# Moving an FFN down product from TensorE to VectorE, with a new start and a re-cut weight stream, in a fused attention and FFN kernel

## Chip, cores and metric

The kernel runs on one core of one Trainium2 chip. The metric is the device time of one execution in microseconds (us). The kernel before takes 263.93 us, the median of 3 runs (263.43 to 264.33).

The engines are named as in the profile: PE is TensorE (PEld its weight loads), DVE is VectorE, ACT is ScalarE, POOL is GpSimd, SP is SyncE, which issues most of the transfers. In the listings "L75" is the line of one helper through which nearly every instruction is issued, so groups are told apart by their tiles (`output<-inputs`) and not by line.

## The reference, cut to what matters

Sequence 2048, width 1024, FFN width 3584, bf16. The output mixes a linear attention block and an FFN that is applied to one single row of x, the one with the largest router logit:

```python
g = sigmoid((x * gate_w).sum(-1))             # one gate per row
pq, pk = phi(x @ Wq), phi(x @ Wk)             # phi(t) = (t > 0 ? t + 1 : exp(t)) + 1e-6
a = (pq @ (pk.T @ v)) / (pq @ pk.sum(0)) @ wo # per head, 32 heads of 32
r = x @ w_r;  i = argmax(r)
h = silu(x[i] @ w_gate) * (x[i] @ w_up)       # 3584 values of one row
b = x;  b[i] += sigmoid(r[i]) * (h @ w_down)
out = g * a + (1 - g) * b
```

Nearly all of the arithmetic is attention. The FFN has almost none, but it moves 22 MB of weights.

## The kernel before: the parts that matter here

PE takes its work in program order: the start (two x tiles transposed, first K products), K and V for x tiles 0 to 3, router product, then for each of the x tiles 4 to 15 a K pair, a V pair, the accumulation of K'V (`kvacc`, 8 small matmuls) and some Q units. FFN weight tiles are slipped in between. A "unit" is eight 128x512 matmuls into one of four PSUM work buffers.

```python
Q_PER_T = {4: 2, 5: 1, 6: 1, 7: 2, 8: 1, ...}
FFN_PER_T = {6: 8, 8: 8, 10: 8, 12: 8, 13: 1, 14: 7, 15: 7}  # weight tiles after x tile t
FFN_DEPTH = 10                                # weight tiles in flight

# the start (abridged): K weights of 512 columns in four pieces, then the rest
load_x(0, 1); load_w0(0); load_x(1, 1)
for c2 in range(1, 4): load_w0(c2)
load_x(2, 2)
for nb in range(1, 4): load_wkv(nb)

# FFN gate and up: the row stands in column 0 of a padded 128x32 weight;
# four column groups of the array each take 512 of the 2048 columns of a tile
for j in range(nr):                           # nr = 4, in the second half 3
    pe.matmul(ps[32*j : 32*j+32, :], lhsT=xs_pad[:, c, :],
              rhs=wt[:, 512*j : 512*j+512], ..., tile_position=(0, 32*j))

# FFN down: 28 row blocks x 4 column groups = 112 matmuls of 256 columns
pe.matmul(ps[32*j : 32*j+32, :], lhsT=hT_pad[:, k, :],
          rhs=wt[:, 1024*kk + 256*j : 1024*kk + 256*j + 256], start=(k == 0), stop=(k == 27), ...)

# gate logits to token columns: four fp32 products with a selection matrix
pe.matmul(gl_ps[:, 4*b : 4*b+4], lhsT=rg_f[:, b*P : (b+1)*P], rhs=selg[:], ...)

# copy of x (4 MB) into the tensor in which the FFN row is replaced later
ffn_prefetch()                                # ten weight tiles
cp = nc.sync.dma_start(out=xp[:], in_=x2d)    # ... then the copy, in the same queue
```

`phi` costs two ACT steps and one DVE step for each K and Q unit; that DVE step is what frees the PSUM buffer.

Of the kernel before, what the change touches and what calls it, by code (L numbers as in the profile page):

```python
# [21 lines left out]
P = 128  # L22
# [8 lines left out]
N_WARM = 7  # L31
Q_PER_T = {4: 2, 5: 1, 6: 1, 7: 2, 8: 1, 9: 1, 10: 2, 11: 1, 12: 1, 13: 2, 14: 1, 15: 0}
FFN_PER_T = {6: 8, 7: 0, 8: 8, 9: 0, 10: 8, 11: 0, 12: 8, 13: 1, 14: 7, 15: 7}
FFN_DEPTH = 10
# [4 lines left out]
def kernel(  # L39
# [66 lines left out]
    ps_acc = ph1.enter_context(tc.tile_pool(name="ps_acc", bufs=1, space=PSUM))  # L106
# [15 lines left out]
    def load_w0(c2):  # L122
        sp.dma_start(out=wkv[:, 2 * c2 : 2 * c2 + 2, 0:512], in_=wqkv_v[:, 2 * c2 : 2 * c2 + 2, D : D + 512])

    def load_wkv(nb):
        sp.dma_start(out=wkv[:, :, 512 * nb : 512 * nb + 512], in_=wqkv_v[:, :, D + 512 * nb : D + 512 * nb + 512])

    load_x(0, 1)
    load_w0(0)
    load_x(1, 1)  # L130
    for c2 in range(1, 4):
        load_w0(c2)
    load_x(2, 2)
    for nb in range(1, 4):
        load_wkv(nb)
# [27 lines left out]
    selg = const.tile([P, 4], F32)  # L163
    nc.gpsimd.memset(selg[:], 0.0)
    for j in range(4):
        nc.gpsimd.memset(sel4[32 * j : 32 * j + 1, j : j + 1], 1.0)
    pidx_i = const.tile([P, 4], I32)
    nc.gpsimd.iota(pidx_i[:], pattern=[[-32, 4]], base=-1, channel_multiplier=1)
# [6 lines left out]
    hT_pad = rt.tile([P, 28, 32], BF)  # L175
    nc.gpsimd.memset(hT_pad[:], 0.0)
# [3 lines left out]
    kvacc = [ps_acc.tile([P, 512], F32, name=f"kvacc{i}") for i in range(3)]  # L180
# [17 lines left out]
    def unit_T(t):  # L198
        xt = xnat[t]
        pst = ps_work.tile([P, D], BF, tag="w")  # L200
        for c in range(KC):
            pe.transpose(pst[:, c * P : (c + 1) * P], xt[:, c * P : (c + 1) * P], ident[:])
        dst = xT[:, :, t * P : (t + 1) * P]
        src = pst[:].rearrange("p (c s) -> p c s", c=KC)
        if t < 3:
            dve.tensor_copy(dst, src)
        else:
            act.copy(dst, src)
# [48 lines left out]
    kv_open(1)  # L257
    unit_T(0)
    warm(3)
    ps0 = ps_work.tile([P, 512], F32, tag="w")  # L260
    kv_mm(ps0, 0, 0, 0, 2)
    unit_T(1)
    ps1 = ps_work.tile([P, 512], F32, tag="w")
    kv_mm(ps0, 0, 0, 2, 4)
    warm(1)
    kv_mm(ps0, 0, 0, 4, 8)
    e00 = phi_exp(ps0[:])
    kv_mm(ps1, 1, 0, 0, 4)
    unit_T(2)
    kv_mm(ps1, 1, 0, 4, 8)  # L270
    unit_T(3)
    e01 = phi_exp(ps1[:])
    phi_dve(ps0[:], e00, pk_t[0][:, 0:512])
    phi_dve(ps1[:], e01, pk_t[1][:, 0:512])
    for t in (2, 3):
        unit_KV(t, 0)
    pidx_f = const.tile([P, 4], F32)
    dve.tensor_copy(pidx_f[:], pidx_i[:])
    dve.tensor_scalar(selg[:], pidx_f[:], 0.0, None, op0=ALU.is_equal)
# [7 lines left out]
    for nb in range(1, 4):  # L287
        for t in range(4):
            unit_KV(t, nb)
# [11 lines left out]
    act.copy(rg_f[:], rps[:])  # L301
    r_f = rt.tile([P, 512], F32)
# [35 lines left out]
    def router_part2():  # L338
        xs_ps = ps_ffn.tile([P, KC + 1], F32, tag="f")
        for c in range(KC):  # L340
            pe.matmul(xs_ps[:, c : c + 1], lhsT=xsel_row[0:1, c * P : (c + 1) * P], rhs=one_bf[0:1, 0:1],
                             start=True, stop=True)
        pe.matmul(xs_ps[:, KC : KC + 1], lhsT=ones_row[0:1, :], rhs=rmax_bf[0:1, 0:1], start=True, stop=True)
        dve.tensor_copy(xs_pad[:, :, 0], xs_ps[:, 0:KC])
        act.activation(sig[:], xs_ps[:, KC : KC + 1], ACTF.Exp, scale=-1.0)
        dve.tensor_scalar_add(sig[:], sig[:], 1.0)
        dve.reciprocal(sig[:], sig[:])
        gl_ps = ps_ffn.tile([P, NT], F32, tag="f")
        for b in range(4):
            pe.matmul(gl_ps[:, 4 * b : 4 * b + 4], lhsT=rg_f[:, b * P : (b + 1) * P], rhs=selg[:], start=True, stop=True)  # L350
        act.activation(gate[:].rearrange("p (j b) -> p j b", b=4), gl_ps[:].rearrange("p (b j) -> p j b", j=4),
                             ACTF.Exp, scale=-1.0)
        dve.tensor_scalar_add(gate[:], gate[:], 1.0)
        dve.reciprocal(gate[:], gate[:])
        dve.tensor_scalar(omg[:], gate[:], -1.0, 1.0, op0=ALU.mult, op1=ALU.add)


# [5 lines left out]
    def ffn_pieces():  # L363
        for half in range(2):
            nr = 4 if half == 0 else 3
            c0 = 2048 * half
            for wi, wmat in enumerate((B_w_gate, B_w_up)):
                wv = wmat.rearrange("(c p) f -> p c f", p=P)
                for c in range(KC):
                    def load(half=half, nr=nr, c0=c0, wv=wv, c=c):  # L370
                        wt = ffw.tile([P, 2048], BF, tag="ffw")
                        ld = nc.sync.dma_start(out=wt[:, 0 : 512 * nr], in_=wv[:, c, c0 : c0 + 512 * nr])  # L372
                        if not ffn_state.get("first"):
                            ffn_state["first"] = True
                            tc.add_manual_dep(ld.ins, xsel_ld[0].ins.name, SYNC, reason="row fetch before the weight stream")
                        return wt

                    def compute(wt, half=half, nr=nr, wi=wi, c=c):
                        if c == 0:
                            ps = ps_ffn.tile([P, 512], F32, tag="f")  # L380
                            ffn_state["ps"] = ps
                            if nr < 4:
                                dve.memset(ps[96:128, :], 0.0)
                        ps = ffn_state["ps"]
                        for j in range(nr):
                            pe.matmul(ps[32 * j : 32 * j + 32, :], lhsT=xs_pad[:, c, :], rhs=wt[:, 512 * j : 512 * j + 512],
                                             start=(c == 0), stop=(c == KC - 1), tile_position=(0, 32 * j))
                        if c == KC - 1:
                            if wi == 0:
                                eg = tmp.tile([P, 512], F32, tag="ffn_e", bufs=1)  # L390
                                act.activation(eg[:], ps[:], ACTF.Exp, scale=-1.0)
                                dve.tensor_scalar_add(eg[:], eg[:], 1.0)
                                dve.reciprocal(eg[:], eg[:])
                                dve.tensor_tensor(sg_t[half][:], ps[:], eg[:], op=ALU.mult)
                            else:
                                dve.tensor_tensor(h_bf[half][:], ps[:], sg_t[half][:], op=ALU.mult)

                                def h_transpose(half=half, nr=nr):
                                    hps = ps_ffn.tile([P, 16], F32, tag="f")
                                    for b in range(4):  # L400
                                        pe.matmul(hps[:, 4 * b : 4 * b + 4], lhsT=h_bf[half][:, b * P : (b + 1) * P],
                                                         rhs=sel4[:], start=True, stop=True)
                                    dst = hT_pad[:, 16 * half : 16 * half + 4 * nr, 0].rearrange("p (j b) -> p j b", b=4)
                                    src = hps[:].rearrange("p (b j) -> p j b", j=4)[:, 0:nr, :]
# [3 lines left out]
                                ffn_state["barrier"] = True  # L408
# [3 lines left out]
        for k2 in range(14):  # L412
            def load(k2=k2):
                wt = ffw.tile([P, 2048], BF, tag="ffw")
                nc.sync.dma_start(out=wt[:].rearrange("p (k n) -> p k n", k=2), in_=wdv[:, 2 * k2 : 2 * k2 + 2, :])
                return wt

            def compute(wt, k2=k2):
                if k2 == 0:
                    ffn_state["ps"] = ps_ffn.tile([P, 256], F32, tag="f", name="yps")  # L420
                ps = ffn_state["ps"]
                for kk in range(2):
                    k = 2 * k2 + kk
                    for j in range(4):
                        pe.matmul(ps[32 * j : 32 * j + 32, :], lhsT=hT_pad[:, k, :],
                                         rhs=wt[:, 1024 * kk + 256 * j : 1024 * kk + 256 * j + 256],
                                         start=(k == 0), stop=(k == 27), tile_position=(0, 32 * j))
                if k2 == 13:
# [10 lines left out]
    def ffn_prefetch():  # L439
        while len(inflight) < FFN_DEPTH:  # L440
            nxt = next(pieces, None)
            if nxt is None:
                return
            inflight.append((nxt[0](), nxt[1]))

    def ffn_step(n):
        pend = ffn_state.pop("pending", None)
        if pend is not None:
            pend()
            if ffn_state.get("stage2_next"):  # L450
                return
        for _ in range(n):
            if not inflight:
# [4 lines left out]
            if ffn_state.pop("barrier", False):  # L458
                ffn_state["stage2_next"] = ffn_state.get("n_h", 0) == 1
                ffn_state["n_h"] = ffn_state.get("n_h", 0) + 1  # L460
                return
# [4 lines left out]
    for t in range(4, NT):  # L466
        for nb in range(4):
            unit_KV(t, nb)
            if nb == 1 and t > 4:
                unit_KVACC(t - 1)  # L470
        nq = Q_PER_T[t]
        for i in range(nq):
            unit_Q(*q_units.popleft())
            if t == 4 and i == 0:
                router_part1()
                ffn_prefetch()
                cp = nc.sync.dma_start(out=xp[:], in_=x2d)
                tc.add_manual_dep(cp.ins, xsel_ld[0].ins.name, SYNC, reason="row fetch before the copy")
        if t == 5:
            router_part2()  # L480
        if t >= 6:
            ffn_step(FFN_PER_T[t])
# [148 lines left out]
```

## Time and profile before

| before | |
|---|---|
| time, median of 3 | 263.93 us |
| span of the profiled execution | 263.1 us |
| PE busy | 257.7 us, 98% |
| DVE busy | 116.1 us, 44% |
| PE waits for FFN weights | 0.6 us |

The prediction below shows the lines that carry this. Groups of PE instructions of the kernel before by shape (count | busy us, mean ns of one | idle before them):

```profile
L75 PE MATMUL ps<-wt,xs_pad 128*32 128x512 bf16 x112 | 8.0, 381 | 0.6 <-DMA wt<-in_B_w_gate_dram 0.4 <-DMA wt<-in_B_w_up_dram 0.2
L75 PE MATMUL yps<-wt,hT_pad 128*32 128x256 bf16 x112 | 3.4, 273 | 0.0
```

The busy column is the union of overlapping matmuls, which is why 112 matmuls of 381 ns each make 8.0 us. A better measure of a part, on an engine that never stops, is the distance between the start of one row of its timeline and the start of the next.

For comparing whole runs I cut the span at two PE rows: the start ends where the router product (`rps`) starts, the middle ends where the first product of denominators (`dps`) starts.

### The profile page before, as it was taken

The numbers are of one execution on the slowest core, as the hardware profiler recorded it, in microseconds if no ns is written. First come the engines' busy times: TensorE is split into PE (matmuls) and PEld (weight loads), VectorE is DVE, ScalarE is ACT, GpSimd is POOL, SyncE is SP. The second block draws the span as 40 slices with busy tenths as digits, with TensorE's granted clock in tenths as the row PEclk, the third lists the DMA queues.
The fourth block names the chain that finished last, engine by engine and source line by source line (L and its number), as shares of the span: only waits on it lengthen the run. The fifth ranks groups of instructions, "written<-read, shape, count | busy, mean of one in ns | idle before, by whom it ended". The sixth has DMA issues, their size and how long they took to land.

```text
span 263.1 us, 4003 instructions
## 1 busy us (share of the span) xinstructions
PE 257.7 (98%) x1541; PEld 122.0 (46%) x1541; DVE 116.1 (44%) x216; ACT 127.5 (48%) x201; POOL 47.9 (18%) x101
## 2 busy tenths in 40 slices
PE   7999999999999999999999999999999999999995
PEld 3444445445444445444444445544444444444443
DVE  1354005233181322328222222276995579964443
ACT  1286324555445534554634545257799751333310
POOL 7000001010000000000000000011997019970000
PEclk9999999999999999999999999999999999999999
DMA  6999990009996997019219807176000274455222
GB/s 175 351 298 208 250 319 0 0 3 340 410 518 230 376 348 298 0 49 362 109 41 302 298 0 267 54 236 226 0 2 0 80 229 149 138 185 159 82 80 80
DMA packets 33058, 47.71 MB, mean 181 GB/s; under 512 B 14152, under 2 KB 18640, under 8 KB 32976
## 3 DMA queue, kind: packets, MB, share of 16 engines
q1 hardware_dynamic: 32752, 47.32, 54.3%
q8 instruction: 12, 0.20, 0.3%
q0 software_dynamic: 256, 0.14, 0.2%
q14 instruction: 6, 0.05, 0.1%
q10 hardware_dynamic: 32, 0.00, 0.0%
HBM read 39.85 MB, written 8.39 MB: 183 GB/s over the span
## 4 chain that ended last, share of the span: by engine, by line
PE 81%; DMA 14%; SPq 2%; issue 0%; DVE 0%
PE ps L75 76%; DMA wt<-in_B_w_up_dram 12%; PE kvacc L75 2%; DMA wkv<-in_A_wqkv_dram 2%; SPq L372 2%; PE yps L75 1%; SPq L75 1%; PE dps L75 1%; PE rps L75 1%; PE pst L75 0%; DVE ot L75 0%; PE pt L75 0%; PE hps L75 0%; PE wps L75 0%
## 5 line engine op out<-in xcount | busy, mean ns | idle before, releaser
L75 PE MATMUL ps<-wkv,xT 128*128 128x512 bf16 x512 | 116.1, 380 | 0.1
L75 PEld LDWEIGHTS <-xT 128*128 128x128 bf16 x512 | 48.8, 98 | 57.0 <-issue 2.3
L75 ACT ACTIVATE u<-ps 128x512 f32<-128x512 f32 x64 | 38.2, 597 | 53.2 <-PE ps L75 52.5
L75 PE MATMUL ps<-xT,wq 128*128 128x512 bf16 x256 | 58.9, 379 | 0.0
L75 PE MATMUL ps<-m_sb,pq_all 128*128 128x512 bf16 (+1 forms) x264 | 55.6, 373 | 0.0
L75 DVE SCALAR_TENSOR_TENSOR pq_all<-ps,e 128x512 bf16<-128x512 f32 x32 | 21.8, 685 | 50.5 <-ACT e L75 50.5
L75 ACT ACTIVATE e<-u 128x512 f32<-128x512 f32 x64 | 40.4, 631 | 1.7
L75 PEld LDWEIGHTS <-pq_all 128*128 128x128 bf16 x264 | 25.8, 98 | 29.8 <-issue 0.4
L75 PEld LDWEIGHTS <-wq 128*128 128x128 bf16 x256 | 24.8, 98 | 29.9 <-issue 0.6
L545 POOL TENSOR_TENSOR pq_all<-pq_all,rb 128x512 bf16<-128x512 bf16 x32 | 36.0, 1170 | 7.4 <-DVE rb L75 7.4
L75 DVE SCALAR_TENSOR_TENSOR pk<-ps,e 128x512 bf16<-128x512 f32 x32 | 21.9, 686 | 32.5 <-ACT e L75 32.5
L75 ACT CAST vt<-ps 128x512 bf16<-128x512 f32 x32 | 18.8, 587 | 32.9 <-PE ps L75 32.9
L75 DVE SCALAR_TENSOR_TENSOR ot<-ps,gate,xg 128x512 bf16<-128x512 f32 (+1 forms) x33 | 23.7, 723 | 16.8 <-PE ps L75 15.0
L75 ACT ACTIVATE xg<-xt,omg 128x1024 f32<-128x1024 bf16 x16 | 18.2, 1147 | 25.9 <-DVE ot L75 25.9
L75 DVE STREAM_SHUFFLE rb<-rdp 128x512 f32<-128x512 f32 x32 | 22.2, 732 | 0.0
L217 POOL MEMSET vt<- 128x8 bf16 x16 | 1.9, 136 | 106.9 <-PE kvacc L75 106.9
L75 PEld LDWEIGHTS <-pk 128*128 128x128 bf16 x128 | 8.5, 98 | 3.3 <-issue 0.4
L75 PE MATMUL kvacc<-vt,pk 128*128 128x129 bf16 x128 | 9.7, 221 | 0.0
L75 ACT CAST m_sb<-ps 128x512 bf16<-128x512 f32 x16 | 9.3, 583 | 0.0
L75 PE MATMUL ps<-wt,xs_pad 128*32 128x512 bf16 x112 | 8.0, 381 | 0.6 <-DMA wt<-in_B_w_gate_dram 0.4
L431 POOL DMA_DIRECT2D xp<-brow x1 | 0.6, 573 | 38.5 <-DVE brow L75 38.5
L75 DVE RECIPROCAL rd<-dn 128x512 f32<-128x512 f32 x2 | 6.7, 3353 | 1.7 <-ACT dn L75 1.7
(99 smaller groups left out, 79.7 us busy)
## 6 DMA issues: line engine op xcount, KB each, us to landing
wt<-in_B_w_down_dram SPq DMA_DIRECT2D x14, 512.0 KB, 7.4
wt<-in_B_w_gate_dram SPq DMA_DIRECT2D x8, 512.0 KB, 8.9
wt<-in_B_w_up_dram SPq DMA_DIRECT2D x8, 512.0 KB, 18.7
xt<-xp SPq DMA_DIRECT2D x16, 256.0 KB, 2.7
out_dram<-ot SPq DMA_DIRECT2D x15, 256.0 KB, 2.0
wkv<-in_A_wqkv_dram SPq DMA_DIRECT2D x3, 1024.0 KB, 11.0
wt<-in_B_w_gate_dram SPq DMA_DIRECT2D x8, 384.0 KB, 5.9
wt<-in_B_w_up_dram SPq DMA_DIRECT2D x8, 384.0 KB, 5.2
```

Of the source, the lines that this page charges most:

```text
L75: inst = fn(*a, **k)
L217: nc.gpsimd.memset(vt_t[t][:, :, 128:129], 1.0)
L372: ld = nc.sync.dma_start(out=wt[:, 0 : 512 * nr], in_=wv[:, c, c0 : c0 + 512 * nr])
L431: nc.gpsimd.dma_start(out=xp[bass.ds(nonlocal_idx[0], 1), :].rearrange("o (j n) -> (o j) n", j=4), in_=brow[0:128:32, :])
L545: nc.gpsimd.tensor_tensor(sl, sl, rb[:], op=ALU.mult)
```

## The change

It does five things: K weights come row by row and serve two x tiles at once from the start; the down product becomes 28 multiply-adds on DVE, with a short fp32 sum over partitions on PE at the end; gate and up use four equal column groups in both halves (512, then 384 columns), four tiles at a time instead of eight; the gate logits reach their token columns through a small DRAM tensor, not through PE; and the copy of x is issued after the last FFN weight. The schedule of the FFN tiles follows (`FFN_PER_T`), with nine weight tiles in flight instead of ten. The aim is to take work off PE, which is busy for 98% of the span.

```diff
-N_WARM = 7
+N_WARM = 5
-FFN_PER_T = {6: 8, 7: 0, 8: 8, 9: 0, 10: 8, 11: 0, 12: 8, 13: 1, 14: 7, 15: 7}
-FFN_DEPTH = 10
+FFN_PER_T = {6: (0, 4), 7: (4, 4), 8: (4, 4), 9: (4, 4), 10: (4, 2), 11: (2, 2), 12: (1, 2), 13: (1, 2), 14: (1, 2), 15: (1, 0)}
+FFN_DEPTH = 9
@@ the start @@
+    def load_k(c):
+        sp.dma_start(out=wkv[:, c, 0:D], in_=wqkv_v[:, c, D : 2 * D])
     load_x(0, 1)
-    load_w0(0)
+    load_k(0)
     load_x(1, 1)
... (six K rows, x tile 2, two K rows, x tile 3, V in two halves)
+    first = [[ps_work.tile([P, 512], F32, tag="w", ...) for nb in range(2)] for t in range(2)]
... (K row c: two matmuls for x tile 0, two for x tile 1; x tiles through a PSUM pool of their own)
@@ gate logits @@
-        for b in range(4):
-            pe.matmul(gl_ps[:, 4 * b : 4 * b + 4], lhsT=rg_f[:, b * P : (b + 1) * P], rhs=selg[:], start=True, stop=True)
+    nc.sync.dma_start(out=gl_d[:], in_=rg_f[1:128:32, :])
+            ld = nc.sync.dma_start(out=gl[:].rearrange("p (j b) -> p j b", b=4), in_=gl_d[:].rearrange("j (b p) -> p j b", p=P))
@@ gate and up @@
-            nr = 4 if half == 0 else 3
-            c0 = 2048 * half
+            w = 512 if half == 0 else 384
+            c0 = 512 * half
-                        ld = nc.sync.dma_start(out=wt[:, 0 : 512 * nr], in_=wv[:, c, c0 : c0 + 512 * nr])
+                        ld = nc.sync.dma_start(out=wt[:, 0 : 4 * w].rearrange("p (j f) -> p j f", j=4),
+                                          in_=wv[:, c, :].rearrange("p (j f) -> p j f", j=4)[:, :, c0 : c0 + w])
@@ down product @@
-                        pe.matmul(ps[32 * j : 32 * j + 32, :], lhsT=hT_pad[:, k, :],
-                                         rhs=wt[:, 1024 * kk + 256 * j : 1024 * kk + 256 * j + 256],
-                                         start=(k == 0), stop=(k == 27), tile_position=(0, 32 * j))
+                    if i2 == 0 and kk == 0:
+                        dve.tensor_scalar(yacc[:], w, h1, None, op0=ALU.mult)
+                    else:
+                        dve.scalar_tensor_tensor(yacc[:], w, h1, yacc[:], op0=ALU.mult, op1=ALU.add)
+                if i2 == 13:
+                    for j in range(4):
+                        pe.matmul(ps[32 * j : 32 * j + 32, :], lhsT=ones_f[:], rhs=yacc[:, 256 * j : 256 * j + 256],
+                                  start=True, stop=True, tile_position=(0, 32 * j))
@@ copy of x @@
             if nxt is None:
+                if not ffn_state.get("copied"):
+                    cp = nc.sync.dma_start(out=xp[:], in_=x2d)
...
-                cp = nc.sync.dma_start(out=xp[:], in_=x2d)
@@ loop over x tiles @@
+            if nb == 1:
+                ffn_step(FFN_PER_T.get(t, (0, 0))[0])
```

In the new `FFN_PER_T` the first number is the tiles taken after the K pair of an x tile, the second those after its Q units.

## The prediction

> **What bounds the kernel now.** I read the busy table first, then the chain of work that ended last, then the waits of the matrix engine (engine, tile, releaser; us in total, times, longest).
>
> ```profile
> PE 257.7 (98%) x1541; PEld 122.0 (46%) x1541; DVE 116.1 (44%) x216; ACT 127.5 (48%) x201; POOL 47.9 (18%) x101
> PE 81%; DMA 14%; SPq 2%; issue 0%; DVE 0%
> ...
> PE ps L75 <- DMA wt<-in_B_w_gate_dram: 0.4, 1, 0.4
> PE ps L75 <- DMA wt<-in_B_w_up_dram: 0.2, 1, 0.2
> ```
>
> PE is busy for 257.7 of 263.1 us and, once started, waits only for FFN weights, twice, 0.6 us in all. The 14% of DMA in the chain is mostly the FFN weight stream, followed back from one of these short waits; it is not 14% that could be won. So time comes only from work taken off PE, from those 0.6 us, and from the first 10 us, where warm-up matmuls count as busy. Any new wait of PE counts in full.
>
> Next the timeline of PE at the parts that the diff touches (start, length in us):
>
> ```profile
> 61.35 1.02 PE L75 MATMUL gl_ps<-selg,rg_f 128*128 128x4 f32 x8
> 62.23 2.97 PE L75 MATMUL ps<-wkv,xT 128*128 128x512 bf16 x13
> ...
> 115.64 1.91 PE L75 MATMUL ps<-wt,xs_pad 128*32 128x512 bf16 x24
> 117.48 3.63 PE L75 MATMUL ps<-wkv,xT 128*128 128x512 bf16 x16
> ...
> 157.78 1.71 PE L75 MATMUL yps<-wt,hT_pad 128*32 128x256 bf16 x56
> 159.42 3.63 PE L75 MATMUL ps<-wkv,xT 128*128 128x512 bf16 x16
> ...
> 166.90 1.71 PE L75 MATMUL yps<-wt,hT_pad 128*32 128x256 bf16 x56
> 168.55 1.68 PE L75 MATMUL ps<-xT,wq 128*128 128x512 bf16 x7
> ```
>
> A part's cost on PE is from its start to the start of the next row: gate logits 0.88 us, eight weight tiles of the second FFN half 1.84 us, the down product 1.64 + 1.65 us. A unit of K, V or Q (eight 128x512 matmuls) costs 1.73 us by the same reading (3.45 for 16).
>
> Then the supply and the vector engine: stretches with GB/s at their end, and two vector groups.
>
> ```profile
> 11.00:17.00 6.00, 6.00 (x41) 3.08 (x40) 2.67 (x4) 4.29 (x8) 0.00 (x0) 1.00 1.09 348
> 60.00:72.00 12.00, 12.00 (x92) 6.06 (x93) 3.19 (x9) 6.17 (x12) 0.13 (x1) 1.00 1.00 396
> ...
> L75 DVE SCALAR_TENSOR_TENSOR pk<-ps,e 128x512 bf16<-128x512 f32 x32 | 21.9, 686 | 32.5 <-ACT e L75 32.5
> L75 DVE TENSOR_TENSOR kvbd<-kvacc,mask_bd 128x384 bf16<-128x384 f32 x2 | 1.1, 547 | 0.0
> ```
>
> The first stretch is K and V weights in runs of 1 KB: 348 GB/s. The second is FFN weights in runs of 4 KB: 396. The engines are saturated in both. The vector rows give the slope of a two-tensor operation: (686 - 547)/128 = 1.09 ns per column.
>
> **What the Trainium skill says.** (1) "VectorE: DVE Perf Modes", sections on the errata and on the tier table: a two-tensor operation with an fp32 operand runs at one element per cycle, and an fp32 add of N columns takes (N + 151)/0.96 ns. That gives 691 ns at 512, against 686 here, so the trace agrees (that row reads one operand from PSUM). (2) "FP8 and Floating Point Precision", TensorE Precision Notes: true fp32 takes four passes. The trace only shows four fp32 products listed as eight matmuls. (3) "DMA: Bandwidth & Descriptors", Specifications: below 512 B per run a transfer is read-modify-write. No run of before has such a load of 4-byte pieces, which the change adds.
>
> **The change, part by part.**
>
> *Down product to VectorE.* Removes 3.29 us of PE. It adds four fp32 matmuls of 256 columns on four column groups. A bf16 group of that size costs 1.64/14 = 0.117 us; four passes, if the groups overlap as now, 0.47, and with weight loads some 0.7. Net on PE: -2.6. On VectorE it adds 28 operations on 1024 columns. By the formula each is (1024 + 151)/0.96 = 1.22 us, 1.25 with the gap to a dependent successor (about 0.04 in the timeline), except the first, which has one tensor and may run twice as fast. Sum 27 x 1.25 + 0.7 = 34.5 us. VectorE is idle for more than that, but only in total; the rival below is about where they fall.
>
> *FFN in four equal groups.* The second half used three column groups of 512 for 1.84 us per eight tiles, as long as four groups would take; now four of 384. Estimated 1.84 x 384/512 = 1.38, twice: -0.9 us.
>
> *Gate logits by way of DRAM.* The four fp32 products go: -0.9 us on PE. A load of 2048 pieces of 4 bytes now stands in the queue before the first FFN weights. I guess 2 us for it; nothing here measures it.
>
> *x copy behind the FFN weights.* 4 MB (8 MB of traffic) leave the busiest stretch of the queues. The copy now starts near 125 us and must end before the FFN row is written near 157; at 400 GB/s it takes about 20, so it is hidden. It should take the 0.6 us of waits with it.
>
> *Start.* Before, both x tiles are transposed and six matmuls done at 9.45 us, and PE doesn't wait after that. In the new order x tile 1 is still the third transfer, landing near 7.3 us; transpose and 0.69 us copy make it usable at 8.75. After that each K row of 256 KB feeds four matmuls, 0.86 us, and arrives every 0.7 us (at 370 GB/s), so PE isn't starved. At 8.8 it has done four matmuls, at 9.2 six: -0.2 us. But now all four PSUM work buffers hold the first two tiles. The last matmul into the first of them ends near 14.4; exp steps (0.60 + 0.63) and the vector step (0.69) free it near 16.4, while PE wants it at 15.7: +0.7. Start in sum: +0.5, within an error of 1.
>
> Sum before new waits: -2.6 - 0.9 - 0.9 - 0.6 + 0.5 = -4.5 us, to 259.4.
>
> **Rivals.**
>
> *Weights come late.* Gate and up tiles are now fetched as four runs of 1 KB (then 768 B) per row, instead of one of 4 KB, so I use 348 GB/s: 1.5 us a tile. From 60 us, with 2 us for the scattered load and 2 us to landing, tile 4 is there at 70.1 and tile 8 at 76.2. PE asks for tiles 1 to 4 at 69.9 (70.78 before, less the gate logits) and for 5 to 8 a K pair later, near 74.7. That is a wait of about 1.5 us; later tiles are asked for at 1.3 us each with nine buffers of lead and come within tenths. Against it: before, eight tiles landed by 72.9, and without the copy the queues are free. If the 4-byte load takes 6 us, this rival costs 5 us; at 396 GB/s and a short load it costs nothing. I take +1.0.
>
> *VectorE becomes the bound of the middle.* The order of the compiled kernel puts the 28 operations from the end of x tile 9 to the end of tile 14, among 17 evacuations of 0.69 us. 34.5 + 11.6 + 1.5 of small ones is 47.6 us of vector work. PE needs for the same stretch 20 K and V units, 7 Q units and 5 accumulations: 27 x 1.73 + 5 x 0.47 = 49 us. The two are nearly level, and VectorE takes them in order, waiting for each weight tile; four in a row hold back a PSUM evacuation by 5 us, which four buffers of 1.73 us barely cover. Walking the order by hand I get PE waits between 0.5 and 3 us, about one for each x tile with a pair of Q units or a run of four. I take +0.5 to 2, middle 1.1. If a vector operation took 1.4 instead of 1.25, VectorE would need 51.6 us and PE would lose 3 to 4 us, and the whole gain of the down product with it.
>
> *The fp32 sum doesn't overlap, or waits for its accumulator.* Then it costs 2 us instead of 0.7: +1.3. Less likely, but possible.
>
> *The copy collides with the end.* If it ran past 157 us, the row, the final x tiles and the output weights would all be late. 30 us of room against 20 speak against it.
>
> **Range and chances.** 259.4 + 1.0 + 1.1 = 261.5 by the median route. The schedule constants are visibly chosen to pace these tiles (4, 4, 2 and 1 at a time), which speaks for waits at the low end, so I put the time at 260.7. No waits and a start 1 us better gives 258; both rivals in full give 264. Two per cent faster is 258.65, which needs nearly every part to go well: 0.20. Slower by 2% would take a long scattered load or a vector jam: 0.03.
>
> **What will show it.** No yps rows of 56 matmuls, instead four to eight fp32 ones within 1 us. FFN rows of 384 columns at about 1.4 us per eight tiles. Waits of PE for the weight tiles of 1 to 2 us near 75 us. VectorE busy over 90% from about 108 to 155 us and total busy near 150; its 1024-column rows at 1.2 us; PE idle there for vector evacuations 0.5 to 2 us. From the start, the first K units all done (64 matmuls and four transposes) near 22.6 us. I am wrong if the scattered load holds the queue for over 4 us, if vector steps pass 1.4 us, or if the first 20 us change by more than 1 us.

## The result, and the profile after

The changed kernel takes 261.35 us, median of 4 runs (260.98 to 261.43); the kernel before 263.78 us in 4 runs (263.43 to 264.33). The ratio is 0.990, 95% interval 0.988 to 0.992: faster by 1%, which counts as the same at a threshold of 2%. A ratio here is always the mean time of one kernel's fast runs over that of the other's of the same rounds, so it is not quite the ratio of the medians quoted. All were fast runs, with a mean granted clock of 0.999 or 1.

The page of the kernel after (busy line, then the chain that ended last, shares by engine), and the waits of PE:

```profile
PE 251.2 (97%) x1413; PEld 117.3 (45%) x1440; DVE 147.4 (57%) x241; ACT 126.0 (49%) x200; POOL 47.0 (18%) x99
PE 70%; DVE 14%; DMA 7%; issue 4%; SPq 3%; ACT 0%; POOLq 0%; DVEq 0%; POOL 0%
...
PE ps L75 <- DVE pk L75: 0.9, 2, 0.5
PE first L75 <- DVE xT L75: 0.6, 2, 0.4
PE ps L75 <- DMA wt<-in_B_w_gate_dram: 0.3, 1, 0.3
```

DVE went from 116.1 to 147.4 us and now stands on the chain with 14%. PE waits twice for a vector step that frees a PSUM buffer, a wait that the kernel before did not have: 0.55 us of the 0.9 lie in the new start (at 15.03 us), only 0.31 (at 143.84) among VectorE's new work. It still waits once for an FFN weight. The drop of PE from 257.7 to 251.2 us busy is larger than the gain: some records of matmuls are missing from the trace (1413 of them stand against 1440 weight loads; before it was 1541 and 1541).

The timeline of PE at the parts that the diff touches (start, length in us, operation, count, wait before it):

```profile
15.03 7.07 PE L75 MATMUL ps<-wkv,xT 128*128 128x512 bf16 x32 [0.55 <-DVE pk L75]
...
75.03 0.40 PE L75 MATMUL ps<-wt,xs_pad 128*32 128x512 bf16 x4 [0.32 <-DMA wt<-in_B_w_gate_dram]
...
87.38 1.05 PE L75 MATMUL ps<-wt,xs_pad 128*32 128x512 bf16 x16
88.36 3.63 PE L75 MATMUL ps<-wkv,xT 128*128 128x512 bf16 x16
...
94.17 0.83 PE L75 MATMUL ps<-wt,xs_pad 128*32 128x384 bf16 x16
94.94 3.19 PE L75 MATMUL ps<-wkv,xT 128*128 128x512 bf16 x14
...
143.84 3.75 PE L75 MATMUL ps<-xT,wq 128*128 128x512 bf16 x16 [0.31 <-DVE pk L75]
...
156.80 0.64 PE L75 MATMUL yps<-yacc,ones_f 128*32 128x256 f32 x8
157.37 3.63 PE L75 MATMUL ps<-wkv,xT 128*128 128x512 bf16 x16
```

Four tiles of 512 columns take 0.98 us from start to start (87.38 to 88.36), four of 384 take 0.77. The fp32 sum takes 0.57 us where the two old blocks took 1.64 and 1.65.

VectorE: its new group (27 operations, 34.6 us busy, 1281 ns each), its timeline around the first of them, and three stretches (busy us of PE, PEld, DVE, ACT and POOL with counts, then granted clock, DMA share, GB/s):

```profile
L75 DVE SCALAR_TENSOR_TENSOR yacc<-wt,hcol,yacc 128x1024 f32<-128x1024 bf16 x27 | 34.6, 1281 | 0.5
...
108.72 0.75 DVE L75 TENSOR_SCALAR yacc<-wt,hcol 128x1024 f32<-128x1024 bf16 x1 [5.05 <-DMA wt<-in_B_w_down_dram]
109.39 0.68 DVE L75 SCALAR_TENSOR_TENSOR pq_all<-ps,e 128x512 bf16<-128x512 f32 x1
...
60.00:72.00 12.00, 11.89 (x72) 5.40 (x72) 3.11 (x7) 5.82 (x12) 0.13 (x1) 1.00 1.06 322
72.00:75.00 3.00, 2.71 (x27) 1.36 (x26) 0.89 (x2) 2.24 (x4) 0.13 (x1) 1.00 1.09 348
130.00:150.00 20.00, 19.64 (x100) 9.22 (x101) 19.75 (x23) 10.43 (x19) 0.13 (x1) 1.00 0.31 106
```

From 130 to 150 us DVE is busy for 19.75 us of 20. Before that it stands idle for 5.05 us, waiting for the first down weight, with the evacuation at 109.39 queued behind that wait. And the weight stream runs at 322 GB/s from 60 to 72 us, where it ran at 396 before. Both means include the first 2 us of the stream, which after the change stands behind the small load (179 GB/s from 60 to 62 us). In full flow it is 348 GB/s, which is the rate that the prediction took for runs of 1 KB, against 403 to 424 before (62 to 72 us).

The prediction read from one execution of the kernel before, which was one of its slower ones (264.65 us). So I took the kernel before and the kernel after once more with a profile (experiments `before_again` and `control_again`, below):

| profiled execution | time | start | middle |
|---|---|---|---|
| before, first | 264.65 | 37.09 | 136.35 |
| before, again | 263.03 | 36.09 | 135.74 |
| after, first | 260.98 | 36.06 | 133.58 |
| after, `control` | 260.72 | 36.43 | 132.92 |
| after, again | 260.35 | 36.35 | 132.62 |

The cuts are these rows, of `before_again` first and then of the kernel after (router product, denominators):

```profile
36.09 1.91 PE L75 MATMUL rps<-xT,wrg_pad 128*32 128x512 bf16 x32
171.83 1.05 PE L75 MATMUL dps<-pq_all,zc 128*32 128x512 bf16 x16
```

```profile
36.06 1.91 PE L75 MATMUL rps<-xT,wrg_pad 128*32 128x512 bf16 x32
169.64 1.05 PE L75 MATMUL dps<-pq_all,zc 128*32 128x512 bf16 x16
```

The first pair of traces would have credited the start with 1.03 us. The second takes that away: the start of the same program differs by 1 us between executions. The two traces of the kernel before also show where most of it lies, first trace and second:

```profile
6.52 1.05 PE L75 MATMUL ps<-wkv,xT 128*128 128x512 bf16 x2
7.38 0.65 PE L75 MATMUL pst<-ident,xnat 128*128 128x128 bf16 x8
```

```profile
6.25 0.59 PE L75 MATMUL ps<-wkv,xT 128*128 128x512 bf16 x2
6.69 0.61 PE L75 MATMUL pst<-ident,xnat 128*128 128x128 bf16 x8
```

From start to start, the same two matmuls take 0.86 us in the first and 0.44 in the second. The clock record in the traces begins, at its full value, at 7.44 us in the first and at 5.97 in the second, so PE comes to full rate 1.5 us later in the first; at half rate that costs some 0.7 us (an estimate from these numbers). The mean clock of 1.00 hides this, because time without a record counts in it as full. What is left of the gain lies in the middle, 2.2 to 3.7 us by the pair one chooses.

### The profile page after: what moved, and what is told of

It reads as the page before. It is cut to its first block, busy times and chain, and to the rows that moved or that the text cites. A ratio compares the mean times of both kernels' runs of the same rounds, so it can differ in the third digit from the quotient of the medians.

```text
span 259.4 us, 3816 instructions
## 1 busy us (share of the span) xinstructions
PE 251.2 (97%) x1413; PEld 117.3 (45%) x1440; DVE 147.4 (57%) x241; ACT 126.0 (49%) x200; POOL 47.0 (18%) x99
## 4 chain that ended last, share of the span: by engine, by line
PE 70%; DVE 14%; DMA 7%; issue 4%; SPq 3%; ACT 0%; POOLq 0%; DVEq 0%; POOL 0%
PE ps L75 62%; DVE yacc L75 10%; DMA wt<-in_B_w_gate_dram 3%; SPq L388 3%; DMA wt<-in_B_w_down_dram 3%; PE first L75 2%; PE kvacc L75 2%; DVE pk L75 1%; DVE pq_all L75 1%; PE pst L75 1%; PE warm_ps L75 1%; DVE xT L75 1%; PE dps L75 1%; DMA xsel<-in_A_x_dram 1%; PE rps L75 1%
## 5 line engine op out<-in xcount | busy, mean ns | idle before, releaser
L75 PE MATMUL ps<-wkv,xT 128*128 128x512 bf16 x465 | 107.2, 379 | 1.5 <-DVE pk L75 0.5
L75 ACT ACTIVATE u<-ps 128x512 f32<-128x512 f32 x60 | 35.8, 596 | 40.7 <-PE ps L75 38.5
L75 DVE SCALAR_TENSOR_TENSOR yacc<-wt,hcol,yacc 128x1024 f32<-128x1024 bf16 x27 | 34.6, 1281 | 0.5
L75 DVE SCALAR_TENSOR_TENSOR pk<-ps,e 128x512 bf16<-128x512 f32 x28 | 19.2, 687 | 22.5 <-ACT e L75 22.5
L75 DVE STREAM_SHUFFLE rb<-rdp 128x512 f32<-128x512 f32 x32 | 22.8, 762 | 0.0
L75 DVE COPY xT<-pst 128x1024 bf16<-128x1024 bf16 x4 | 2.8, 691 | 10.2 <-PE pst L75 10.2
L75 PE MATMUL first<-wkv,xT 128*128 128x512 bf16 x31 | 7.7, 380 | 0.6 <-DVE xT L75 0.6
```

Of the source, the lines that this page charges most:

```text
L75: inst = fn(*a, **k)
```

## The experiments

The theory after the first look: the gain is the down product (less what VectorE gives back) and the gate logits; the four even groups and the start give nothing; and weights that arrive late and VectorE's order cost about 2 us that a better version could have. The rivals are told in each expectation. Eleven runs were made in three sets; each set has its own runs of the kernel before (medians 263.60, 263.86 and 263.51 us, 11 runs each).

### control: the kernel after, unchanged

> The changed kernel again, unedited, as the measure for the other runs. Ratio to before 0.990 (0.988 to 0.992). In its profile the row FFN matmuls of 384 columns near 0.77 us per four tiles, the first accumulation of the down product on VectorE waiting for its weights until about 108.7 us, the 1024-column operation at 1.28 us. The two traces so far differ by 3.7 us, the medians by 2.4; if a second trace of this kernel comes out near 260.5 us instead of 259.4, the spread of single executions explains that.

Measured: 261.33 us (260.72 to 261.94, 6 runs), ratio 0.991 (0.988 to 0.994). The result repeats, with a spread of 1.2 us.

### long_runs: each FFN weight row as one run of 4 KB

```diff
-            c0 = 512 * half
+            c0 = 2048 * half
-                        ld = nc.sync.dma_start(out=wt[:, 0 : 4 * w].rearrange("p (j f) -> p j f", j=4),
-                                          in_=wv[:, c, :].rearrange("p (j f) -> p j f", j=4)[:, :, c0 : c0 + w])
+                        ld = nc.sync.dma_start(out=wt[:, 0 : 4 * w], in_=wv[:, c, c0 : c0 + 4 * w])
-        pairs = [(7 * j + b, 1) for b in (0, 2) for j in range(4)]
-        pairs += [(7 * j + 4, 1) for j in range(4)] + [(6, 7), (20, 7)]
+        pairs = [(2 * i, 1) for i in range(14)]
```

The columns of the FFN are taken in another order, which changes no result; the loads of the first half are then runs of 4 KB instead of four of 1 KB, those of the second 3 KB instead of four of 768 B. (The scatter into `hcol` follows.)

> Only the columns of the FFN are dealt out otherwise: each half is a contiguous block of columns (4 KB, then 3 KB per row), cut into four groups after loading; same bytes, same matmuls, same order on every engine. Theory A (the short runs slow the weight stream to 325 GB/s, so the first down weights come at 108.7 us, VectorE stands 5 us waiting for them and then holds back PSUM for the rest of the stretch): the stream from 60 to 72 us at 390 GB/s or more, no wait of PE for gate weights, first down accumulation at 105 us or before, PE from the start of x tile 10 to the fp32 sum in 50 us instead of 51.5; time 1 to 1.5 us below the changed kernel, ratio to before 0.984 to 0.987. Rival B (the stream is set by buffers coming free, or VectorE has too much work wherever it starts): time within 0.4 us of the changed kernel, PE waits unchanged.

Measured: 259.91 us (259.47 to 260.34), ratio 0.985 (0.982 to 0.988): 1.4 us better than `control` in the same set by the medians, with intervals that just meet. Its weight stream, its issue of the down weights and its first vector accumulation (stretches and timelines of `long_runs`):

```profile
60.00:72.00 12.00, 12.00 (x77) 5.47 (x75) 3.28 (x7) 5.98 (x11) 0.13 (x1) 1.00 1.01 373
72.00:75.00 3.00, 3.00 (x33) 1.52 (x31) 0.69 (x1) 2.32 (x4) 0.13 (x1) 1.00 1.02 408
...
100.54 23.51 SPq L429 DMA_DIRECT2D wt<-in_B_w_down_dram  x14
...
107.97 0.75 DVE L75 TENSOR_SCALAR yacc<-wt,hcol 128x1024 f32<-128x1024 bf16 x1 [4.43 <-DMA wt<-in_B_w_down_dram]
```

In full flow the stream is faster, 408 GB/s against 348. No wait of PE for a weight is listed, but none is listed for `control` either. What the traces do show is the stretch of PE from the accumulation of x tile 6 to that of tile 7, where the wait at 75 us lies: 12.99 us here, and 13.50, 13.30 and 13.13 in the three traces of the kernel after. The part of the theory that the first accumulation would then come early failed: 107.97 us against 108.72 in the first trace of the kernel after and 108.47 in `control`. Nor did PE get faster from the accumulation of x tile 10 to the fp32 sum: 35.73 us in `control`, 35.69 here. The first down load is issued at 100.54 us (101.79 in the first trace of the kernel after) and lands some 7 us later. That the buffers coming free set that time, and not the rate of the stream, is argued and not tested alone. So VectorE's backlog was not cured by this edit, and the part of its gain that the traces show, 0.1 to 0.5 us, lies in waits for weights. The profiled executions of `control` and `long_runs` differ by 0.4 us, and they are one of the fastest of the first and the slowest of the second. Where the rest of the 1.4 us lies is open; that the other runs of the kernel after wait longer for weights than its profiled ones is a guess that no trace shows.

### down_pe: the down product back on PE, the rest as after

```diff
-                        dve.tensor_scalar(yacc[:], w, h1, None, op0=ALU.mult)
-                    else:
-                        dve.scalar_tensor_tensor(yacc[:], w, h1, yacc[:], op0=ALU.mult, op1=ALU.add)
...
+                        pe.matmul(ps[32 * j : 32 * j + 32, :], lhsT=hT_pad[:, k, :],
+                                  rhs=wt[:, 1024 * kk + 256 * j : 1024 * kk + 256 * j + 256],
+                                  start=(i2 == 0 and kk == 0), stop=(i2 == 13 and kk == 1), tile_position=(0, 32 * j))
```

> The changed kernel with the down product back on PE (28 times four bf16 matmuls of 256 columns into PSUM), all else as changed. Theory A (the move saves 3.29 - 0.57 = 2.7 us of PE, and vector operations in the way of evacuations cost 1.6 us of it): this is 1.1 us slower than the changed kernel, ratio to before 0.994; VectorE total busy near 113 us, PE from x tile 10 to the end of x tile 14 without waits. Rival B (the waits in that stretch have another cause and stay): 2.7 us slower, ratio 1.000. Rival C (VectorE work costs as much as it saves): same time as changed.

Measured: 264.79 us (264.24 to 265.45), ratio 1.004 (1.001 to 1.007): 3.46 us worse than `control`, more than any of the three theories allowed. One of its blocks in the timeline of PE:

```profile
131.85 0.64 PE L75 MATMUL kvacc<-vt,pk 128*128 128x129 bf16 x8
132.42 0.40 PE L75 MATMUL yps<-wt,hT_pad 128*32 128x256 bf16 x8
132.75 3.63 PE L75 MATMUL ps<-wkv,xT 128*128 128x512 bf16 x16
```

The accumulation of eight takes 0.47 us by itself, so two row blocks of the down product cost 132.75 - 131.85 - 0.47 = 0.43 us, and not 2 x 0.117 = 0.23. The 0.2 beyond is paid at each entry and exit of such a block. Blocks of four row blocks cost 0.65 us by the same reading, so one row block is 0.11 us and the fixed part of a block 0.21. In the kernel before the 28 row blocks stood in two groups and cost 3.48 us (3.29 by the rows shown, and the gap ahead of each). Under the new schedule they stand in nine and cost 28 x 0.11 + 9 x 0.21 = 5.0 us. This gives VectorE's price as well: with 5.0 us less 0.67 for the fp32 sum, moving the product should gain 4.3 us if VectorE cost nothing; it gained 3.46; so VectorE takes back about 0.8. That is rough, because the two ratios are known to some 0.8 us each.

### start_only: the kernel before with the new start alone

The edit is the whole start of the changed kernel, put into the kernel before. Its core:

```diff
-N_WARM = 7
+N_WARM = 5
-    load_w0(0)
+    load_k(0)
     load_x(1, 1)
-    for c2 in range(1, 4):
-        load_w0(c2)
-    load_x(2, 2)
-    for nb in range(1, 4):
-        load_wkv(nb)
+    for c in range(1, 6):
+        load_k(c)
...
```

> The kernel before with only the new start (K rows loaded whole, two x tiles at once, transposes evacuated by VectorE, 7 warm-up matmuls). Theory A (the start is worth 1.0 us, as the router product begins at 36.06 instead of 37.09 us): router product at 36.1 us, ratio to before 0.996. Rival B (that microsecond is lost again at the first FFN weights, whose arrival is tied to the router and the copy): router product at 36.1 us but ratio within 0.001 of 1, with longer waits of PE for gate weights near 72 us.

Measured: 263.83 us (263.16 to 264.56), ratio 1.0002 (0.997 to 1.003). No gain is seen, within some 0.8 us. Its router product starts at 36.71 us, not at 36.1 as both theories had it. Over the eleven traces with the new start it starts at 36.06 to 36.73, and in the two with the old one at 36.09 and 37.09, so the 1.03 us of the first pair of traces was scatter.

This trace shows one thing more: PE's wait of 0.5 us for `DVE pk` is there although the down product is still on PE, so it belongs to the new start.

### before_again and control_again: one more look at each

No edit; one execution with a profile each, on the same chip. Only their traces are used, for the table above.

> The kernel before, unedited, for a second trace. The run with only the new start took as long as before, yet the first traces put the router product 1.0 us earlier after the change. Theory: the first trace of before was of a slow execution (264.65 us against a median of 263.6), so a second one shows the router product at 36.3 to 36.8 us and the stretch from there to the denominators near 135.6 to 136.4 us. Rival: it shows 37.1 us again, and the new start does win a microsecond that start_only lost elsewhere.

> The changed kernel, unedited, for a third trace. The two traces so far are of its fastest executions (260.98 and 260.72 against medians of 261.35 and 261.33). Expected: router product between 36.0 and 36.7 us, PE waiting 0.2 to 1.5 us for the gate weights near 75 us, and the stretch from x tile 10 to the fp32 sum in 50.9 to 51.5 us whatever the rest does.

Measured: 263.03 and 260.35 us. Start 36.09 against 36.35, middle 135.74 against 132.62. The start is level, and the middle carries the whole gain of that pair, 3.1 us. In these two executions PE waits for weights 0.2 us or less. Cut finer, at PE's accumulations: 0.88 us are gained between those of x tiles 4 and 5 (the gate logits), nothing between those of 5 and 12, where all gate and up weights are used (75.45 us before, 75.47 after), and 2.26 us from there to the denominators (the down product, less what VectorE costs).

### half_acc: half of VectorE's new work, on top of long_runs

```diff
-                for kk in range(2):
+                for kk in range(1):
```

Half of the down product is left out, so the result is wrong. (The comparison with the reference did not notice: only one of 2048 rows is touched.) The loads stay.

> long_runs with every second accumulation of the down product left out, wrong on purpose: 14 instead of 28 vector operations of 1.28 us, everything else the same. Theory A (VectorE is full from 109 to 154 us and holds back PSUM): the stretch of PE from x tile 10 to the fp32 sum falls from 50.9 to 50.0 us, the time by 0.9 us against long_runs, ratio to before 0.981 to 0.983. Rival B (the microsecond is lost to the order, a few operations in a row ahead of an evacuation, not to the amount): the stretch stays above 50.6 us and the ratio at 0.985.

Measured: 259.27 us (259.06 to 259.72), ratio 0.983 (0.981 to 0.985). Against `long_runs` of another set, by the ratios, that is 0.2%, about 0.5 us, so the timing alone hardly tells them apart. The traces do. These are rows of PE's timeline in `long_runs`, then in `half_acc`: the accumulation of x tile 10 and the fp32 sum.

```profile
120.45 0.64 PE L75 MATMUL kvacc<-vt,pk 128*128 128x129 bf16 x8
156.14 0.64 PE L75 MATMUL yps<-yacc,ones_f 128*32 128x256 f32 x8
```

```profile
120.76 0.64 PE L75 MATMUL kvacc<-vt,pk 128*128 128x129 bf16 x8
155.55 0.64 PE L75 MATMUL yps<-yacc,ones_f 128*32 128x256 f32 x8
```

PE does the same work in between: 35.69 us with all 28 operations, 34.79 with 14. So VectorE costs PE 0.9 us there, near the 0.8 that `down_pe` gives by another way. (By the same rows the other traces of the kernel after take 36.21, 35.73 and 35.61 us.) In `long_runs` none of it is a listed wait of PE for VectorE in that stretch. It is spread over short pauses: four rows of 16 matmuls take 3.68 to 3.75 us there, and 3.61 or 3.62 in `half_acc`.

### gates_pe: the gate logits back on PE

```diff
-    nc.sync.dma_start(out=gl_d[:], in_=rg_f[1:128:32, :])
-            ld = nc.sync.dma_start(out=gl[:].rearrange("p (j b) -> p j b", b=4), in_=gl_d[:].rearrange("j (b p) -> p j b", p=P))
+        for b in range(4):
+            pe.matmul(gl_ps[:, 4 * b : 4 * b + 4], lhsT=rg_f[:, b * P : (b + 1) * P], rhs=selg[:], start=True, stop=True)
```

> The changed kernel with the gate logits transposed by four fp32 products on PE again, as before, and no load of 4-byte pieces ahead of the FFN weights. Theory A (the products cost 0.88 us of PE and the scattered load delays nothing that PE waits for): 0.9 us slower than the changed kernel, ratio to before 0.994 to 0.995. Rival B (the scattered load, 2.9 us from issue to landing, holds up the first weights): weights come 1 to 2 us earlier, the wait near 75 us goes, and the time is within 0.4 us of the changed kernel.

Measured: 261.70 us (261.01 to 262.87), ratio 0.993 (0.990 to 0.996), against 0.991 for `control` in the other set: 0.4 to 0.5 us worse, with intervals that overlap, so the timing alone shows no difference. In the traces both theories hold a part. PE spends its 0.9 us again. But the FFN's weights then start earlier, and the wait in the second block of weights, which is 0.32 us in the kernel after, is gone. The stretch between the accumulations of x tiles 6 and 7 takes 13.00 us, where the three traces of the kernel after have 13.13 to 13.50. So of the 0.9 us that the removed products save, 0.1 to 0.5 are given back. The load of 2048 pieces takes 2.9 us from issue to landing in the kernel after (I had guessed 2 for its hold on the queue).

### copy_early: the copy of x ahead of most FFN weights

```diff
-                    cp = nc.sync.dma_start(out=xp[:], in_=x2d)      # after the last weight
+                cp = nc.sync.dma_start(out=xp[:], in_=x2d)          # after the first nine weights
+                ffn_state["last_ld"] = cp
```

> The changed kernel with the 4 MB copy of x back in its old place, behind the first nine weight tiles instead of behind all of them. Theory A (the even schedule asks for weights as fast as the queues bring them, 1.3 us a tile, so 8 MB of copy traffic ahead of tile 10 shows on PE): PE waits 8 to 12 us in all for up and gate weights between 82 and 110 us, time 269 to 273 us, ratio to before 1.02 to 1.035. Rival B (the copy is hidden by the nine buffers, as it was in before): PE waits under 1 us, ratio within 0.003 of the changed kernel's 0.991.

Measured in three rounds: 273.41 us (270.86 to 274.60, 4 runs), ratio 1.038 (1.034 to 1.043), worse than the theory's upper end. The waits of PE and one stretch of `copy_early`:

```profile
PE ps L75 <- DMA wt<-in_B_w_up_dram: 8.1, 3, 6.3
...
80.00:90.00 10.00, 3.16 (x19) 1.01 (x17) 1.88 (x3) 2.46 (x4) 0.00 (x0) 0.73 0.87 300
```

PE waits 8.1 us for weights, 6.3 of it in one piece. The loss is larger than that, because the clock goes as well. From the accumulation of x tile 6 to that of tile 7 this trace, of the fastest of the four executions, takes 10.5 us longer than `long_runs`, 8.1 of them listed waits; by the medians the whole loss is 12 us. The mean granted clock is 0.73 in this stretch and 0.76 in the next; cut finer, it is 0.50 from 84.5 to 94.8 us. The Trainium skill says in "TensorE: Matmul & The Clock Gate", Part 1, that PE falls to half clock after an idle window of about 3.4 us. The half clock agrees; the delay does not, because the fall came 2.0 us after PE's last matmul (82.55 us). So with the spread schedule and nine buffers the copy had to move, while in the kernel before, where it stood behind ten tiles, PE waited only 0.6 us for weights.

### blocks8: eight tiles at a time again, ten in flight, on top of long_runs

```diff
-FFN_PER_T = {6: (0, 4), 7: (4, 4), 8: (4, 4), 9: (4, 4), 10: (4, 2), 11: (2, 2), 12: (1, 2), ...}
-FFN_DEPTH = 9
+FFN_PER_T = {7: (8, 0), 8: (8, 0), 9: (8, 0), 10: (8, 2), 11: (2, 2), 12: (1, 2), ...}
+FFN_DEPTH = 10
```

> long_runs with the gate and up tiles taken eight at a time again (after the K pairs of x tiles 7, 8, 9 and 10) instead of four at a time, and ten buffers. Theory A (each block of 32-column matmuls between full ones costs PE a fixed 0.21 us beyond its matmuls; four blocks fewer): the stretch from accumulation 5 to accumulation 10 on PE falls from 57.0 us in long_runs by 0.8 us, time 0.5 to 0.8 us below long_runs, ratio to before 0.982 to 0.983. Rival B (eight at a time asks for weights before they have landed): PE waits for weights 1 us or more, and the time is that of long_runs, 0.985, or above.

Measured: 258.97 us (258.63 to 260.09), ratio 0.983 (0.979 to 0.987), correct. It beats both kernels, the one after by 0.8% (by the two ratios of different sets); whether it is 2% faster than the kernel before is unclear, as the interval includes 0.98. Against `long_runs` it gains 0.5 us by the ratios and 0.9 by the medians, and 1.8 us in the middle of the two traces, that of `long_runs` being of its slowest execution. In the traces two things account for it. First, four blocks fewer: from the accumulation of x tile 5 to that of tile 10 PE takes 119.82 - 63.73 = 56.09 us here and 120.45 - 63.49 = 56.96 in `long_runs`, so 0.87 us for four blocks, 0.22 each. Second, VectorE costs nothing any more. PE's rows in `blocks8`, the same two as above:

```profile
119.82 0.64 PE L75 MATMUL kvacc<-vt,pk 128*128 128x129 bf16 x8
154.61 0.64 PE L75 MATMUL yps<-yacc,ones_f 128*32 128x256 f32 x8
```

That is 34.79 us, what `half_acc` took, but with all 28 operations. Here is VectorE in `blocks8`, up to its first accumulation:

```profile
105.43 0.69 DVE L75 SCALAR_TENSOR_TENSOR pq_all<-ps,e 128x512 bf16<-128x512 f32 x1 [2.00 <-ACT e L75]
107.16 0.69 DVE L75 SCALAR_TENSOR_TENSOR pk<-ps,e 128x512 bf16<-128x512 f32 x1 [1.03 <-ACT e L75]
108.61 0.75 DVE L75 TENSOR_SCALAR yacc<-wt,hcol 128x1024 f32<-128x1024 bf16 x1 [0.77 <-DMA wt<-in_B_w_down_dram]
```

The first accumulation starts as late as before, so the tenth buffer brought the weight no earlier. But the Q evacuation of x tile 9 and the first K evacuation of tile 10 now stand ahead of it in the queue, not behind it, so VectorE waits 0.77 us for the weight instead of 5.05 (4.43 in `long_runs`) and starts without those two in arrears. From there to its last evacuation before the fp32 sum it then works for 44.6 us, where `long_runs` takes 45.8. The amount of work is the same, so the amount alone was not the cost. The traces point to the order around one late weight, on an engine with no slack to make it up. `blocks8` changes the blocks, the order and the depth together, though, and no run changes the order alone.

### blocks8_mixed: the last four of the 28 row blocks on PE, on top of blocks8

```diff
+                    if i2 >= 12:
+                        for j in range(4):
+                            pe.matmul(ffn_state["ps"][32 * j : 32 * j + 32, :], lhsT=hT_pad[:, k - 24, :],
+                                      rhs=w[:, 256 * j : 256 * j + 256],
+                                      start=(i2 == 12 and kk == 0), stop=False, tile_position=(0, 32 * j))
```

The fp32 sum then adds to the same PSUM tile. (`FFN_PER_T` gets 14: (0, 3) instead of (1, 2), so that these four come last.)

> blocks8 with the last 4 of the 28 row products of the down projection on PE as bf16 matmuls in the same block as the fp32 sum, so 24 vector operations. Theory A (VectorE holds back PE by 0.9 us, and 5 us less work frees most of it, while 16 bf16 matmuls cost 0.47 us): 0.2 to 0.4 us below blocks8. Rival B (the waits come from runs of four operations, not from the sum): 0.3 to 0.5 us above blocks8.

Measured: 259.26 us (259.00 to 260.40), ratio 0.984 (0.980 to 0.987), correct: 0.3 us slower than `blocks8` by the medians, inside the intervals, as rival B had it. There was no wait left to free. The two rows of the product in PE's timeline:

```profile
154.68 0.62 PE L75 MATMUL yps<-wt,hT_pad 128*32 128x256 bf16 x16
155.13 0.60 PE L75 MATMUL yps<-yacc,ones_f 128*32 128x256 f32 x8
```

The 16 matmuls cost 0.45 us, and nothing was seen to pay for them.

## Why the prediction was right, step by step

The predicted 260.7 us against 261.35 measured is inside the range, and "within 2%" had the largest chance. But some terms were wrong and cancelled, which is luck: the one gain that did not come (0.9 us, four groups) was made up by costs that did not come either (0.5, start; in the traces, half or more of the 1.0 for new waits). The sum of the terms was 261.5, nearer to the result than the 260.7 to which it was shaded.

| term of the sum | predicted | measured | by |
|---|---|---|---|
| down product off PE | -2.6 | -2.8 | 3.48 before, 0.67 after, each with its entry |
| VectorE as the bound | +1.1 | +0.8 to +0.9 (1.4 in the first trace) | `down_pe`, `half_acc` |
| gate logits off PE | -0.9 | -0.9, less 0.1 to 0.5 given back | `gates_pe`, traces |
| four even groups | -0.9 | 0.0 | block times, `blocks8` |
| weight waits, old ones gone and new ones come | -0.6 + 1.0 | listed waits 0.6 before, 0.3 after, in the first traces; open in the timed runs | traces, `long_runs` |
| start | +0.5 | 0.0 | `start_only` |

**Down product.** Right in mechanism and size. The fp32 sum was estimated at 0.7 us with weight loads and took 0.57 by its rows, 0.67 with its entry. The rival that it would take 2 us is refuted.

**VectorE.** Right in size, and right on what the profile would show: over 90% busy in the middle, 147.4 us in total against "near 150". The other sign, PE idle for vector evacuations for 0.5 to 2 us, came only in sum: the list of waits shows 0.31 us in that stretch of the first trace and nothing in the other two (the 0.5 us at 15 us is the start's), and the 0.9 us appear when whole stretches are compared. The operation took 1281 ns where the formula and the gap gave 1.25 us. The reason was given as too much work in too little time. `half_acc` agrees with that, and `blocks8` shows that it is not the whole of it: there the same work costs PE nothing, with two evacuations ahead of a late weight.

**Four groups: the step that failed.** It said "now four of 384. Estimated 1.84 x 384/512 = 1.38, twice: -0.9 us." The scaling by columns is right for the matmuls and leaves out the change of block size that came with it. A block costs its matmuls plus a fixed part. By the rows, with 0.10 us for the gap ahead of each block, eight tiles of 512 took 1.94 us before, and four tiles of 512 now take 1.08 and four of 384 take 0.87. The difference of the first two is 0.215 us a tile, which leaves 0.22 for the block; `down_pe` gave 0.21. So before, 4 x 1.94 = 7.76 us; after, 4 x 1.08 + 4 x 0.87 = 7.80. The narrower columns save 0.8 us and four more blocks spend it. The sign named for it, "about 1.4 us per eight tiles", showed 2 x 0.77 us. The Trainium skill says in "TensorEngine Tiling (Array Packing)", Key Properties, that changing the tiling mode drains TensorE. These blocks are the places where PE goes from full-width to 32-column matmuls and back, and a fixed cost would fit that; no run isolates the drain itself.

**Gate logits.** The 0.9 us on PE is right, the guess of 2 us for the scattered load was near (2.9 from issue to landing), and 0.1 to 0.5 us of the gain goes to it. This was foreseen as part of the rival of late weights.

**Late weights.** The rival came, smaller in the traces than drawn: 0.32 us at 75 us where 1.5 was computed, 0.1 to 0.5 by the stretch from accumulation 6 to 7. The rate was right (348 GB/s); but the small load was issued at 57.89 us, and tile 8 was there at 75.03, not at 76.2. `long_runs` gains 1.4 us in timed runs by removing the short runs, but only this much of it is found in a trace, so whether +1.0 was a fair size is not shown.

**Start.** Predicted +0.5 within 1, measured 0. The PSUM wait that it named exists (0.55 us at 15.03), but x tile 1 was transposed at 5.98 us, earlier than the 7.3 assumed for its landing. The tell-tale "if the first 20 us change by more than 1 us" would have misled: one execution of the same kernel differs from another by that much.

**The copy.** It started at 124.76 us and was hidden, as predicted; the DMA engines are at rest from 136 us, after 11 us and not 20. `copy_early` shows that putting it back ahead of the weights costs 12 us under this schedule, which the prediction did not ask.

In sum, by the traces of `before_again` and `control_again`: -2.8 + 0.9 - 0.9 + 0 = -2.8, against 3.1 us seen in the middle. The medians of the timed runs differ by 2.3 to 2.4 us. The gaps between these three numbers are as large as the scatter of single executions, and stay open.

## What to carry to other kernels

When a stage is cut into more and smaller pieces, count the entries: a piece costs its matmuls plus a fixed part, and doubling the entries can eat what narrower pieces save. An engine that works in order pays for a late operand with everything queued behind it, so on a nearly full engine try the short evacuations that free buffers ahead of the first operation that waits for a transfer (here two of them, and 0.9 us of PE, though no run changed this alone). And profile a kernel twice before crediting a part of a change with 1 us: here the start of one unchanged program differed by that much between two executions.

## What the Trainium skill lacked or had wrong

- "TensorEngine Tiling (Array Packing)", Key Properties, says that a change of tiling mode drains TensorE, but not what it costs. Here each block of 32-column matmuls among full-width ones costs 0.21 us beyond its matmuls, and four blocks fewer gain 0.87 us.
- "DMA: Bandwidth & Descriptors" tabulates bandwidth by the size of a transfer. For this chip it does not compare runs of different length above 512 B: transfers of the same 512 KB ran at 348 GB/s in runs of 1 KB and at 408 in runs of 4 KB (72 to 75 us). Nor has it a duration for a small load of 4-byte pieces: 2048 of them took 2.9 us from issue to landing.
- "VectorE: DVE Perf Modes" gives its formula for the fp32 `tensor_tensor` add, and none for the multiply-add of two tensors and a column. Carried over to 1024 columns the formula gives an estimate of 1.22 us; the multiply-add with a bf16 weight and an fp32 accumulator in SBUF took 1.281. The one-tensor form with bf16 in and fp32 out took 0.75.
